# Filling a kernel's ramp with dummy matmuls, two elevenths of the first input on the instruction rings, weight sums on VectorE, and the last tile's store on its own queue

## The chip, the cores and the metric

The kernel runs on one core of a Trainium2 chip (trn2). The time is the device time of one execution in microseconds; a quoted time is a median over several executions. On one core all runs of this study were in the ordinary (fast) state, so no slow runs enter. A trace comes from one profiled execution, whose span is about 1.7 us shorter than the device time of the same run; positions in time ("at 15.4") are microseconds from the start of that trace.

The engines are TensorE (PE in the profile; PEld is its weight load), VectorE (DVE), ScalarE (ACT), GpSimd (POOL) and SyncE (SP). SP, ACT and POOL each issue DMAs on a queue of their own; those of SP and ACT are called the instruction rings here. Input 0 is divided into eleven groups for loading, its "elevenths". The matmuls write to tiles in PSUM, a memory that this program divides into eight banks; a "tag" is a pool of it with a fixed number of buffers.

## The reference

For each of 8 inputs of 2496 x 256: a real Fourier transform over the sequence, a complex 256 x 256 product with bias, a soft threshold, the inverse transform; then a mixture of experts that picks one expert per input and applies two matrix products.

```python
X = np.fft.rfft(x, axis=1)                       # 8 x 2496 x 256
Yr = X.real @ w_r - X.imag @ w_i + b_r
Yi = X.real @ w_i + X.imag @ w_r + b_i
Yr = sign(Yr) * maximum(abs(Yr) - 0.01, 0)       # Yi the same
y  = np.fft.irfft(Yr + 1j * Yi, n=2496, axis=1)
e_idx = argmax(y.mean(axis=1) @ w_gate, axis=1)  # one expert for each input
out = gate_w * (maximum(y @ w1[e], 0) @ w2[e])
```

## The kernel before

Everything is laid out by a small list scheduler inside the kernel: every operation is given a cost and a virtual time, and the scheduler emits the instructions of each engine in the order that its model finds best. It is a model; on the chip the order stays as emitted, whatever the real times are.

The parts that the change touches, with cuts:

```python
BANKS = {"a": 5, "h": 2, "o": 1}          # PSUM banks for each tag: "o" has one
...
warm = cpool.tile([P, 512], FP16, name="warm")
nc.vector.memset(warm, 0.0)
x0_part(nc.sync, 0, 0, 2, xf)             # input 0, elevenths 0-1, instruction rings
x0_part(nc.scalar, 1, 0, 2, xf)
x0_part(nc.sync, 2, 0, 2, xf)
nc.scalar.dma_start(out=wa, in_=d_wa.ap())
x0_part(nc.sync, 0, 2, 4, xf)             # elevenths 2-3, instruction rings
...
for c0, c1 in ((4, 8), (8, 11)):          # the rest: GpSimd's queue, casting DMA
    for j in range(3):
        x0_part(nc.gpsimd, j, c0, c1, xin0)
...                                       # w_r and w_i behind it, same queue
pw = psum.tile([P, 512], FP32, tag="o", name="po", bufs=BANKS["o"])
for _ in range(WARM):                     # WARM = 9: raise TensorE's clock
    nc.tensor.matmul(pw, warm[:, 0:P], warm)
...
def bank(nm, tag):                        # a NEW buffer of the tag at each call
    return psum.tile([P, 512], FP32, tag=tag, name=nm, bufs=BANKS[tag])
...
def w_products(_):                        # the sums of the complex product
    nc.gpsimd.tensor_sub(out=w4[:, :, 0], in0=wm, in1=wr)
    nc.gpsimd.tensor_scalar_mul(out=wr, in0=wr, scalar1=-1.0)
    nc.gpsimd.tensor_sub(out=w4[:, :, 1], in0=wr, in1=wm)
```

Names in the profile: `pa` is the first transform stage (from `xin`, evacuated to `XB`), `pm` the "weight product" in the frequency domain of the first two inputs (a transform stage against the weights), `Pt`/`pb` what follows, `z`, `cl`, `Y` VectorE's bias and soft threshold, `pv` and `pi` the inverse transform, `ph` and `po` the two products of the expert, `ost` the output tile. The first two inputs go through this way, the other six through a slightly different one.

Of the kernel before, what the change touches and what calls it, by code (L numbers as in the profile page):

```python
# [11 lines left out]
FP32 = mybir.dt.float32  # L12
AFT = mybir.ActivationFunctionType
ALU = mybir.AluOpType
# [3 lines left out]
B = 8  # L18
# [69 lines left out]
PEN = 0.2  # L88
SLACK = 2.5


class Op:
    def __init__(self, engs, occ, lat, emit, vt, deps, allocs, dma):
        self.engs, self.occ, self.lat, self.emit = engs, occ, lat, emit
        self.vt, self.deps, self.allocs, self.dma = vt, deps, allocs, dma
        self.done = self.after = None
        self.slack = SLACK

# [8 lines left out]
class Schedule:  # L107
# [54 lines left out]
    def run(self):  # L162
        free = dict.fromkeys(("PE", "ACT", "DVE", "SP", "POOL"), 4.0)
        free["POOL"] = 17.0
        ring = {"SP": 7.0, "POOL": 25.0}
        todo = sorted(self.ops, key=lambda o: o.vt)
        self.log = []
        while todo:
            best = None
            seen = {e: 0 for e in free}  # L170
            for o in todo:
                if all(seen[e] > 24 for e in o.engs):
                    continue
                r = self.ready(o)
                if r is None:
                    continue
                for e in o.engs:
                    seen[e] += 1
                    s = max(r, free[e])
                    if e == "DVE" and len(o.engs) > 1:  # L180
                        s += PEN
                    k = (s, o.vt, s + o.lat[e])
                    if best is None or k < best[0]:
                        best = (k, o, e)
            (s, _, _), o, e = best
            if e == "DVE" and len(o.engs) > 1:
                s -= PEN
            todo.remove(o)
            for k in o.allocs:
                self.hist.setdefault(k.tag, []).append(k)  # L190
            free[e] = s + o.occ[e]
            o.done = s + o.lat[e]
            if o.dma:
                other = "POOL" if e == "SP" else "SP"
                t = max(ring[e], s + 1.3)
                behind = max(0.0, ring[other] - t)
                if e == "SP":
                    ext = min(2.3 * o.dma, behind)
                    ring[other] += ext / 2.3
                else:  # L200
                    ext = min(0.43 * o.dma, behind)
                    ring[other] += min(2.3 * behind, o.dma)
                ring[e] = t + o.dma + ext
                o.done = ring[e] + o.slack
            self.log.append((s, e, o))
            o.emit(e)
# [3 lines left out]
def kernel(  # L210
# [29 lines left out]
    XROW = 2 * D + 16  # L240
    WARM = 9
    BUFS = {"XT": 2, "hs": 2, "z": 3, "V": 6}
# [19 lines left out]
    def load_now(b, cuts, hold=None):  # L262
# [18 lines left out]
        "p g c -> p (g c)")[:, 0 : NG * D].rearrange("p (g c) -> p g c", c=2 * D)  # L281
    xf = hpool.tile([117, 4, 2 * D], FP32, name="hs")
    xv = x[0].rearrange("(a n) c -> a n c", n=N2)
    XH = ((0, 2), (2, 4))

# [7 lines left out]
    nc.vector.memset(warm, 0.0)  # L293
    x0_part(nc.sync, 0, 0, 2, xf)
    x0_part(nc.scalar, 1, 0, 2, xf)
    x0_part(nc.sync, 2, 0, 2, xf)
    nc.scalar.dma_start(out=wa, in_=d_wa.ap())
    x0_part(nc.sync, 0, 2, 4, xf)
    x0_part(nc.scalar, 1, 2, 4, xf)
    x0_part(nc.sync, 2, 2, 4, xf)  # L300
    for c0, c1 in ((4, 8), (8, 11)):
        for j in range(3):
            x0_part(nc.gpsimd, j, c0, c1, xin0)
# [3 lines left out]
    nc.gpsimd.dma_start(out=wm, in_=w_i.rearrange("(t p) c -> p t c", p=P))  # L307

    pw = psum.tile([P, 512], FP32, tag="o", name="po", bufs=BANKS["o"])
    for _ in range(WARM):  # L310
        nc.tensor.matmul(pw, warm[:, 0:P], warm)
    tf = cpool.tile([P, NK1, P], FP16, name="tf")
# [20 lines left out]
    e0 = cpool.tile([P, 1], FP16, name="e0")  # L333
    nc.sync.dma_start(out=e0, in_=d_e0.ap())
    wg = cpool.tile([P, 2, E], FP32, name="wg")
    nc.sync.dma_start(out=wg, in_=moe_w_gate.rearrange("(t p) e -> p t e", p=P))
    iot = cpool.tile([P, E], FP32, name="iot")
    nc.sync.dma_start(out=iot, in_=d_iota.ap())
    wi = cpool.tile([120, 117], FP16, name="wi")
    nc.sync.dma_start(out=wi, in_=d_wi.ap())  # L340
    wg16 = cpool.tile([P, 2, E], FP16, name="wg16")
    xin1 = load_now(1, (0, NG // 2))


    X0_AT, X1_AT = (4.3, 5.6, 8.8, 10.5), 25.0
    W_AT, T_AT = 11.2, (13.0, 15.5, 18.0)

# [5 lines left out]
    COPY = {"ACT": nc.scalar.copy, "DVE": nc.vector.tensor_copy}  # L353
    DIRECT = 2
    HOLD = 9
    LATE = -0.12
    PERIOD, SPAN, SHIFT = 49.5, 1.4, 0.6

    def bank(nm, tag):
        return psum.tile([P, 512], FP32, tag=tag, name=nm, bufs=BANKS[tag])  # L360
# [14 lines left out]
    def w_products(_):  # L375

        nc.gpsimd.tensor_sub(out=w4[:, :, 0], in0=wm, in1=wr)
        nc.gpsimd.tensor_scalar_mul(out=wr, in0=wr, scalar1=-1.0)
        nc.gpsimd.tensor_sub(out=w4[:, :, 1], in0=wr, in1=wm)
    w_late = S.op("POOL", 4.0, w_products, 1.0, deps=list(w_in))  # L380

    def wg_cast(eng):
        COPY[eng](out=wg16, in_=wg)
    wg_in = S.evac(20, wg_cast, 0.5, deps=[S.fixed(12.0)])
    t_in = [S.fixed(T_AT[0 if k1 < 4 else 1 if k1 < 12 else 2])
# [5 lines left out]
    def x_cast(c):  # L391
        def emit(eng):
            COPY[eng](out=xin0[:, c], in_=xf[:, c])
        return S.evac(500, emit, -30 + c, deps=[S.fixed(X0_AT[c // 2])])

    x_cast_ops = [x_cast(c) for c in range(4)]
    c1, c2 = [S.fixed(X0_AT[2])], [S.fixed(X0_AT[3])]
    xdone = {0: [x_cast_ops[:2], x_cast_ops[2:], c1, c1, c2, c2],
             1: [S.fixed(X1_AT)]}
# [499 lines left out]
    def add_moe(b, y_ops, yk, gate):  # L899
        w, gb_op, wk = gate  # L900
        v0 = b * PERIOD
        for c, (ns, nl) in enumerate(NCH):
# [32 lines left out]
            for sp in range(2):  # L935
                tago = "o" if b < B - 1 else "h"
                ok = S.tok(tago, BANKS[tago])
                oc = {}
                for q in range(4):
                    v = v0 + PERIOD * (c * 8 + 6 + 4 * sp + q) / 44  # L940

                    def mm(_, sp=sp, q=q, nl=nl, cell=cell, oc=oc, tag=tago):
                        if q == 0:
                            oc["p"] = bank("po", tag).rearrange(
                                "p (i c) -> p i c", i=2)
                        i = q // 2
                        s0 = min((2 * sp + i) * P, nl - P)
                        for ft in range(4 * (q % 2), 4 * (q % 2) + 4):
# [7 lines left out]
                             after=m2 if q else None,  # L956
                             allocs=[ok] if q == 0 else [])
                    m2 = m
                    hk.rel.append(m)
                    wk.rel.append(m)  # L960

                def ev(eng, oc=oc):
# [4 lines left out]
                    else:  # L967
                        nc.vector.tensor_scalar_mul(out=ost, in0=oc["p"],
                                                    scalar1=gbc_t[b])
                e = S.evac(560, ev, v, deps=[m2, gb_op])  # L970
                ok.rel.append(e)

                def st(_, ns=ns, nl=nl, sp=sp, oc=oc):
# [7 lines left out]
                    else:  # L981
# [3 lines left out]
                                          in_=ost[64:P, 1, :])  # L985
                S.op("SP", 0.3, st, v, deps=[e], dma=0.75)

# [34 lines left out]
```

## Time and profile before

| | before |
|---|---|
| time, median (range) | 441.28 us (441.0 to 441.76) |
| TensorE busy | 424.7 us, 96% of the span |
| first weight product of input 0 starts | 15.37 |
| tenth z (input 0 through the threshold) | 36.12 |
| first weight product of input 1 | 39.38 |
| first expert product | 57.15 |
| last matmul ends, kernel ends | 437.2, 441.3 |

These positions are starts read from the timeline.

The busy time of each engine by windows, before. Each line has the window, its length, then busy time and (in brackets) instruction count of TensorE, its weight load, VectorE, ScalarE and GpSimd, then the granted TensorE clock, the DMA share and the rate:

```profile
core 0: us, PE busy (x) PEld busy (x) DVE busy (x) ACT busy (x) POOL busy (x), PEclk, DMA share, GB/s
0.00:12.00 12.00, 6.03 (x31) 2.84 (x32) 1.98 (x5) 3.48 (x5) 6.57 (x15) 0.87 0.81 169
12.00:20.00 8.00, 6.99 (x42) 4.36 (x41) 3.15 (x6) 5.64 (x14) 7.50 (x12) 0.56 0.98 314
...
60.00:441.00 381.00, 375.93 (x3056) 272.39 (x3053) 250.44 (x512) 286.87 (x552) 21.99 (x32) 1.00 0.78 180
```

After 60 us TensorE has hardly a gap (375.9 of 381). What can be gained lies in the first 60 us and in the tail. From 12 to 20 us the granted clock is 0.56 on average.

TensorE in the first 16 us, before (start, length, engine, line and operation, tiles, count; the bracket is the idle time ahead of it and what ended it):

```profile
1.31 4.02 PE L311 MATMUL po<-warm 128*128 128x512 f16 x9 [1.31 <-DVE warm L293]
7.62 0.59 PE L478 MATMUL pa<-wa,xin 117*128 117x120 f16 x8 [2.29 <-ACT xin L393]
10.58 3.78 PE L478 MATMUL pa<-wa,xin 117*128 117x120 f16 x36 [2.37 <-DVE xin L393]
15.37 1.01 PE L514 MATMUL pm<-w,XB 128*128 128x512 f16 x2 [1.01 <-ACT w L364]
```

Nine dummies run from 1.31, done by 5.3, and then TensorE waits for data. The clock goes up at 5.35 and falls back at 8.76, so the first weight products run at half clock. That gap is what the change wants to fill.

The timeline of VectorE, and then that of GpSimd, from 19 to 25 us, before:

```profile
...
20.30 0.37 DVE L565 TENSOR_SCALAR cl<-z 128x512 f16<-128x512 f16 x1
20.71 0.80 DVE L567 TENSOR_TENSOR Y<-z,cl 128x512 f16<-128x512 f16 x1
...
22.36 1.26 DVE L565 TENSOR_SCALAR cl<-z 128x512 f16<-128x512 f16 x1
...
```

```profile
...
19.21 1.30 POOL L377 TENSOR_TENSOR w<-ost 128x512 f16<-128x512 f32 x1
20.61 1.51 POOL L378 TENSOR_SCALAR ost<-ost 128x512 f32<-128x512 f32 x1
22.21 1.26 POOL L379 TENSOR_TENSOR w<-ost 128x512 f16<-128x512 f32 x1
```

While GpSimd makes the weight sums, one `cl` takes 1.26 us and one `Y` 0.80; undisturbed ones take 0.29 and 0.42.

The end of the chain of waits, before (start, length, what; ACTq is ScalarE's sequencer, "issue" a time in which the engine waited for nothing that the profile shows):

```profile
435.95 1.22 PE po L949 x11
437.17 0.03 ACTq L965
437.19 0.05 issue
437.24 0.69 ACT ost L965
```

After the last matmul there is one cast of 0.69 us, then two stores; the span ends 4.1 us after the last matmul.

### The profile page before, as it was taken

What the parts mean: (1) busy time and instruction counts of PE and PEld (TensorE: products, weight loads), DVE (VectorE), ACT (ScalarE), POOL (GpSimd) and SP (SyncE); (2) the same over time, 40 slices, a digit from 0 to 9 for tenths busy, and PEclk for the clock granted to TensorE, in tenths of its full rate; (3) what the DMA queues carried; (4) which work ended last, traced back from release to release, by engine and by line L of the source; (5) the groups of instructions that cost most, each with busy time, mean ns of one, the idle gap of its engine ahead of it and who ended that gap; (6) DMA issues with size and microseconds to landing.
All of it is one profiled execution on the core that took longest, in us unless ns stands there. A gap on an engine that the chain in (4) does not pass through costs nothing.

```text
span 441.3 us, 9023 instructions
## 1 busy us (share of the span) xinstructions
PE 424.7 (96%) x3387; PEld 300.9 (68%) x3387; DVE 288.9 (65%) x605; ACT 328.6 (74%) x636; POOL 45.2 (10%) x69
## 2 busy tenths in 40 slices
PE   4888999999999999999999999999999999999996
PEld 1555566677677866778677876778667787676764
DVE  1496965298866787687966887678976877322110
ACT  2787887777967778777867778677777778678674
POOL 5920300021000200020000200020000010000000
PEclk8698999999999999999999999999999999999999
DMA  7998996899979988699988999699978456472222
GB/s 166 276 183 176 170 211 162 239 207 206 202 230 213 186 174 220 199 199 215 189 256 193 177 189 220 219 199 197 188 211 230 127 134 126 130 161 67 71 73 91
DMA packets 98961, 80.31 MB, mean 182 GB/s; under 512 B 8000, under 2 KB 91889, under 8 KB 98917
## 3 DMA queue, kind: packets, MB, share of 16 engines
q1 hardware_dynamic: 75499, 58.17, 48.9%
q0 software_dynamic: 23184, 21.22, 30.3%
q8 instruction: 26, 0.43, 0.4%
q10 hardware_dynamic: 234, 0.35, 0.3%
q14 instruction: 18, 0.15, 0.1%
HBM read 59.36 MB, written 38.80 MB: 222 GB/s over the span
## 4 chain that ended last, share of the span: by engine, by line
PE 77%; DVE 9%; DMA 7%; ACT 3%; issue 2%; SPq 1%; POOL 0%; ACTq 0%; POOLq 0%; DVEq 0%
PE po L949 28%; PE ph L917 26%; PE pm L693 8%; PE pi L788 3%; PE pa L591 3%; PE pv L436 3%; DMA xin<-in_x_dram 3%; PE px L655 3%; PE pm L514 2%; DMA V<-scr 2%; DVE z L556 2%; DMA hs<-in_x_dram 2%; DVE Y L567 1%; DVE cl L565 1%; DVE Y L735 1%
## 5 line engine op out<-in xcount | busy, mean ns | idle before, releaser
L929 ACT ACTIVATE hs<-ph 128x512 f16<-128x512 f32 (+1 forms) x296 | 170.2, 592 | 73.6 <-PE ph L917 68.4
L949 PE MATMUL po<-w2s,hs 128*128 128x256 f16 x1280 | 180.6, 272 | 0.0
L917 PE MATMUL ph<-ysb,w1s 128*128 128x512 f16 (+1 forms) x640 | 179.8, 374 | 0.5 <-ACT ysb L809 0.5
L949 PEld LDWEIGHTS <-hs 128*128 128x128 f16 x1280 | 123.3, 98 | 51.7 <-issue 2.2
L917 PEld LDWEIGHTS <-w1s 128*128 128x128 f16 x640 | 61.4, 98 | 21.5 <-issue 0.7
L965 ACT ACTIVATE ost<-po,gbc 128x512 f32<-128x512 f32 x78 | 53.7, 689 | 13.0 <-PE po L949 13.0
L735 DVE TENSOR_TENSOR Y<-z,cl 64x512 f16<-64x512 f16 x120 | 50.4, 420 | 2.8
L707 DVE TENSOR_TENSOR tt<-pm,bias 128x512 f16<-128x512 f32 x60 | 38.6, 684 | 19.4 <-PE pm L693 19.4
L693 PE MATMUL pm<-w,XT 128*128 128x256 f16 x360 | 50.0, 273 | 0.4
L693 PEld LDWEIGHTS <-XT 128*128 128x128 f16 x360 | 34.2, 98 | 12.8 <-DVE XT L674 3.8
L931 DVE TENSOR_SCALAR hs<-ph 128x512 f16<-128x512 f32 (+1 forms) x24 | 16.5, 686 | 38.5 <-PE ph L917 33.8
L716 DVE TENSOR_TENSOR z<-pm,tt 128x512 f16<-128x512 f32 x60 | 38.4, 679 | 2.9 <-PE pm L693 2.9
L444 ACT CAST V<-pv 128x512 f16<-128x512 f32 x55 | 32.5, 612 | 2.1 <-PE pv L436 1.5
L803 DVE CAST ysb<-pi 128x468 f16<-128x468 f32 (+1 forms) x41 | 23.0, 582 | 16.8 <-PE pi L788 16.5
L663 DVE CAST XT<-px 128x512 f16<-128x512 f32 x32 | 21.6, 689 | 16.5 <-PE px L655 16.3
L601 ACT CAST A<-pa 120x512 f16<-120x512 f32 x50 | 28.1, 603 | 1.3 <-PE pa L591 1.1
L436 PE MATMUL pv<-Y,ti 128*128 128x256 f16 x160 | 25.9, 272 | 2.5 <-DVE Y L567 2.1
L803 ACT CAST ysb<-pi 128x468 f16<-128x468 f32 (+1 forms) x55 | 25.8, 534 | 2.3 <-PE pi L788 2.2
L514 PE MATMUL pm<-w,XB 128*128 128x512 f16 x80 | 24.7, 428 | 1.9 <-ACT w L364 1.0
L525 ACT CAST Pt<-pm 128x512 f16<-128x512 f32 x35 | 19.9, 589 | 6.7 <-PE pm L514 6.7
L788 PEld LDWEIGHTS <-V 120*128 120x128 f16 x352 | 21.0, 98 | 4.0 <-issue 0.7
L788 PE MATMUL pi<-wi,V 120*128 120x117 f16 x352 | 23.2, 214 | 0.3
(70 smaller groups left out, 332.8 us busy)
## 6 DMA issues: line engine op xcount, KB each, us to landing
out_dram<-ost SPq DMA_DIRECT2D x72, 256.0 KB
scr<-V SPq DMA_DIRECT2D x80, 128.0 KB
V<-scr SPq DMA_DIRECT2D x24, 420.0 KB
xin<-in_x_dram POOLq DMA_DIRECT2D x21, 429.0 KB, 9.3
XB<-fwd SPq DMA_DIRECT2D x30, 256.0 KB
fwd<-A SPq DMA_DIRECT2D x18, 360.0 KB
w1s<-in_moe_w_dram POOLq DMA_DIRECT2D x8, 512.0 KB, 8.3
w2s<-in_moe_w_dram POOLq DMA_DIRECT2D x8, 512.0 KB, 7.8
```

What stands on the lines that cost most here:

```text
L436: nc.tensor.matmul(pv[:, D * i : D * i + D], ti[:, k0 + i, :], cell["Y"](i))
L514: nc.tensor.matmul(pm, A_t[b]["A"][:, ch, k1, :, :], w4[:, ch, 2:4, :].rearrange("p t c -> p (t c)"), start=(ch == 0), stop=(ch == 1))
L693: nc.tensor.matmul(pm[:, D * a : D * a + D], cell["X"][:, ch, a, t].rearrange("p i k -> p (i k)"), w4[:, ch, t, :], start=(ch == 0), stop= ...
L707: nc.vector.tensor_add(out=cell["tt"][:, r], in0=cell["T", 2].rearrange("p (a c) -> p a c", a=2), in1=bias[:, r].unsqueeze(1).to_broadcast ...
L716: nc.vector.tensor_add(out=cell["z"][:, r], in0=cell["T", 1 - r].rearrange("p (a c) -> p a c", a=2), in1=cell["tt"][:, r])
L735: nc.vector.tensor_sub(out=Y[64 * r : 64 * r + 64, :, i], in0=cell["z"][s, r], in1=cell["cl"][s, r])
L788: nc.tensor.matmul(pi[:, 117 * i : 117 * i + M], V2[:, g, ch * P : ch * P + P], w)
L803: COPY[eng](out=yv[:, :, 12 * gb : 12 * gb + 3 * nf].rearrange("p a (g j) -> p a g j", j=3), in_=pi[:, 0 : 117 * nf].rearrange("p (g a j) ...
L917: nc.tensor.matmul(ph[:, 0:nl], w1s_t[b][:, ch, fc * P : fc * P + P], ysb_t[b][:, ch, ns : ns + nl], start=(ch == 0), stop=(ch == 1))
L929: nc.scalar.activation(out=o, in_=i, func=AFT.Relu)
L949: nc.tensor.matmul(oc["p"][:, i, :], cell["hs"][:, ft, s0 : s0 + P], w2s_t[b][:, ft, :], start=(ft == 0), stop=(ft == E - 1))
L965: nc.scalar.activation(out=ost, in_=oc["p"], func=AFT.Copy, scale=gbc_t[b])
```

## The change

Its intent has four parts: (1) only two elevenths of input 0 stay on the instruction rings and the rest comes in one ordered stream on GpSimd's queue; (2) the scheduler may put dummy matmuls into any gap of TensorE until 50 us, so that the clock stays up; (3) the weight sums move from GpSimd to VectorE; (4) the last output tile is cast in halves, by VectorE and ScalarE, and ScalarE's queue issues its last store. The core of the diff, with cuts:

```diff
-    WARM = 9
+    XF = 2
+    X0_CUTS = ((2, 6), (6, 9), (9, 11))
...
-    x0_part(nc.sync, 0, 2, 4, xf)
-    x0_part(nc.scalar, 1, 2, 4, xf)
-    x0_part(nc.sync, 2, 2, 4, xf)
-    for c0, c1 in ((4, 8), (8, 11)):
+    nc.scalar.copy(out=warm[0:1, 0:1], in_=warm[0:1, 1:2])
+    for c0, c1 in X0_CUTS:
...
-    pw = psum.tile([P, 512], FP32, tag="o", name="po", bufs=BANKS["o"])
-    for _ in range(WARM):
-        nc.tensor.matmul(pw, warm[:, 0:P], warm)
...
-        nc.gpsimd.tensor_sub(out=w4[:, :, 0], in0=wm, in1=wr)
-        nc.gpsimd.tensor_scalar_mul(out=wr, in0=wr, scalar1=-1.0)
-        nc.gpsimd.tensor_sub(out=w4[:, :, 1], in0=wr, in1=wm)
+        nc.vector.tensor_sub(out=w4[:, :, 0], in0=wm, in1=wr)
+        nc.vector.scalar_tensor_tensor(out=w4[:, :, 1], in0=wr, scalar=-1.0,
+                                       in1=wm, op0=ALU.mult, op1=ALU.subtract)
...
+    for _ in range(WARM):                       # WARM = 100, until 50.0 us
+        def dummy(_):
+            nc.tensor.matmul(bank("po", "o"), warm[:, 0:P], warm)
+        dk = S.tok("o", BANKS["o"])
+        o = S.op("PE", 0.216, dummy, 1e6, allocs=[dk])
+        dk.rel.append(o)
+        o.until = WARM_END
...
+                if last:     # last output tile: own bank for its second half
+                    e = S.op("DVE", 0.45, ev_first, v, deps=[m1, gb_op])
+                    e = S.op("ACT", 0.45, ev_last, v, deps=[m2, e])
```

The scheduler's new cost table also starts its engines at other times, and four small loads move to a later place on SyncE. A new copy of one element on ScalarE brings its table load to the start.

More of the change, by code (lines that the diff above doesn't have):

```diff
@@ L89 @@
 SLACK = 2.5
+IDLE = 0.2
 class Op:
@@ L96, in __init__ @@
         self.done = self.after = None
-        self.slack = SLACK
+        self.slack, self.until = SLACK, None
 class Tok:
@@ L162, in run @@
     def run(self):
-        free = dict.fromkeys(("PE", "ACT", "DVE", "SP", "POOL"), 4.0)
-        free["POOL"] = 17.0
-        ring = {"SP": 7.0, "POOL": 25.0}
+        free = dict.fromkeys(("PE", "ACT", "DVE", "SP", "POOL"), 1.3)
+        free["ACT"], free["POOL"] = 4.5, 17.0
+        ring = {"SP": 7.0, "POOL": 26.0}
         todo = sorted(self.ops, key=lambda o: o.vt)
         self.log = []
-        while todo:
+        while any(not o.until for o in todo):
             best = None
@@ L174, in run @@
                 r = self.ready(o)
-                if r is None:
+                if r is None or (o.until and max(r, free["PE"]) > o.until):
                     continue
@@ L181, in run @@
                         s += PEN
+                    if o.until:
+                        s += IDLE
                     k = (s, o.vt, s + o.lat[e])
@@ L187, in run @@
                 s -= PEN
+            if o.until:
+                s -= IDLE
             todo.remove(o)
@@ L281 @@
         "p g c -> p (g c)")[:, 0 : NG * D].rearrange("p (g c) -> p g c", c=2 * D)
-    xf = hpool.tile([117, 4, 2 * D], FP32, name="hs")
+    xf = hpool.tile([117, 4, 2 * D], FP32, name="hs")[:, 0:XF]
     xv = x[0].rearrange("(a n) c -> a n c", n=N2)
-    XH = ((0, 2), (2, 4))
     def x0_part(eng, j, c0, c1, dst):
@@ L293 @@
     nc.vector.memset(warm, 0.0)
-    x0_part(nc.sync, 0, 0, 2, xf)
-    x0_part(nc.scalar, 1, 0, 2, xf)
-    x0_part(nc.sync, 2, 0, 2, xf)
+    x0_part(nc.sync, 0, 0, XF, xf)
+    x0_part(nc.scalar, 1, 0, XF, xf)
+    x0_part(nc.sync, 2, 0, XF, xf)
     nc.scalar.dma_start(out=wa, in_=d_wa.ap())
-    x0_part(nc.sync, 0, 2, 4, xf)
-    x0_part(nc.scalar, 1, 2, 4, xf)
-    x0_part(nc.sync, 2, 2, 4, xf)
-    for c0, c1 in ((4, 8), (8, 11)):
+    nc.scalar.copy(out=warm[0:1, 0:1], in_=warm[0:1, 1:2])
+    for c0, c1 in X0_CUTS:
         for j in range(3):
@@ L333 @@
     e0 = cpool.tile([P, 1], FP16, name="e0")
-    nc.sync.dma_start(out=e0, in_=d_e0.ap())
     wg = cpool.tile([P, 2, E], FP32, name="wg")
-    nc.sync.dma_start(out=wg, in_=moe_w_gate.rearrange("(t p) e -> p t e", p=P))
     iot = cpool.tile([P, E], FP32, name="iot")
-    nc.sync.dma_start(out=iot, in_=d_iota.ap())
     wi = cpool.tile([120, 117], FP16, name="wi")
-    nc.sync.dma_start(out=wi, in_=d_wi.ap())
     wg16 = cpool.tile([P, 2, E], FP16, name="wg16")
     xin1 = load_now(1, (0, NG // 2))
-    X0_AT, X1_AT = (4.3, 5.6, 8.8, 10.5), 25.0
-    W_AT, T_AT = 11.2, (13.0, 15.5, 18.0)
+    X0_AT, X1_AT = (5.6, 8.0, 9.3, 10.3), 26.0
+    W_AT, T_AT = 11.6, (14.0, 16.2, 18.4)
     S = Schedule()
@@ L354 @@
     DIRECT = 2
+    WARM, WARM_END = 100, 50.0
     HOLD = 9
@@ L375, in w_products, with small_loads @@
     def w_products(_):
-        nc.gpsimd.tensor_sub(out=w4[:, :, 0], in0=wm, in1=wr)
-        nc.gpsimd.tensor_scalar_mul(out=wr, in0=wr, scalar1=-1.0)
-        nc.gpsimd.tensor_sub(out=w4[:, :, 1], in0=wr, in1=wm)
-    w_late = S.op("POOL", 4.0, w_products, 1.0, deps=list(w_in))
+        nc.vector.tensor_sub(out=w4[:, :, 0], in0=wm, in1=wr)
+        nc.vector.scalar_tensor_tensor(out=w4[:, :, 1], in0=wr, scalar=-1.0,
+                                       in1=wm, op0=ALU.mult, op1=ALU.subtract)
+    w_late = S.op("DVE", 1.4, w_products, -24.9, deps=list(w_in))
+    def small_loads(_):
+        nc.sync.dma_start(out=e0, in_=d_e0.ap())
+        nc.sync.dma_start(out=wg, in_=moe_w_gate.rearrange("(t p) e -> p t e", p=P))
+        nc.sync.dma_start(out=iot, in_=d_iota.ap())
+        nc.sync.dma_start(out=wi, in_=d_wi.ap())
+    small = S.op("SP", 1.6, small_loads, -30, deps=[S.fixed(10.0)], lat=4.0)
+    for _ in range(WARM):
[5 more added lines that the diff above has]
+        o.until = WARM_END
     def wg_cast(eng):
         COPY[eng](out=wg16, in_=wg)
-    wg_in = S.evac(20, wg_cast, 0.5, deps=[S.fixed(12.0)])
+    wg_in = S.evac(20, wg_cast, 0.5, deps=[small])
     t_in = [S.fixed(T_AT[0 if k1 < 4 else 1 if k1 < 12 else 2])
@@ L393, in emit @@
             COPY[eng](out=xin0[:, c], in_=xf[:, c])
-        return S.evac(500, emit, -30 + c, deps=[S.fixed(X0_AT[c // 2])])
-    x_cast_ops = [x_cast(c) for c in range(4)]
-    c1, c2 = [S.fixed(X0_AT[2])], [S.fixed(X0_AT[3])]
-    xdone = {0: [x_cast_ops[:2], x_cast_ops[2:], c1, c1, c2, c2],
+        return S.evac(500, emit, -30 + c, deps=[S.fixed(X0_AT[0])])
+    x_cast_ops = [x_cast(c) for c in range(XF)]
+    c1, c2, c3 = ([S.fixed(t)] for t in X0_AT[1:])
+    xdone = {0: [x_cast_ops, c1, c1, c2, c3, c3],
              1: [S.fixed(X1_AT)]}
@@ L937, in add_moe @@
                 ok = S.tok(tago, BANKS[tago])
+                last = b == B - 1 and c == 4 and sp == 1
+                ok2 = S.tok(tago, BANKS[tago])
                 oc = {}
@@ L940, in add_moe, with mm @@
                     v = v0 + PERIOD * (c * 8 + 6 + 4 * sp + q) / 44
-                    def mm(_, sp=sp, q=q, nl=nl, cell=cell, oc=oc, tag=tago):
-                        if q == 0:
-                            oc["p"] = bank("po", tag).rearrange(
-                                "p (i c) -> p i c", i=2)
+                    def mm(_, sp=sp, q=q, nl=nl, cell=cell, oc=oc, tag=tago,
+                           last=last):
+                        if q == 0 or q == 2 and last:
+                            oc["p"] = oc["p", q // 2] = bank(
+                                "po", tag).rearrange("p (i c) -> p i c", i=2)
                         i = q // 2
@@ L956, in add_moe @@
                              after=m2 if q else None,
-                             allocs=[ok] if q == 0 else [])
-                    m2 = m
+                             allocs=[ok] if q == 0 else [ok2]
+                             if q == 2 and last else [])
+                    m1, m2 = (m if q == 1 else m1 if q else None), m
                     hk.rel.append(m)
@@ L969, in ev @@
                                                     scalar1=gbc_t[b])
-                e = S.evac(560, ev, v, deps=[m2, gb_op])
-                ok.rel.append(e)
                 def st(_, ns=ns, nl=nl, sp=sp, oc=oc):
@@ L985, in st, with ev_last, ev_first @@
                                           in_=ost[64:P, 1, :])
-                S.op("SP", 0.3, st, v, deps=[e], dma=0.75)
+                def ev_last(_, ns=ns, nl=nl, sp=sp, oc=oc):
+                    r0 = ns + 256 * sp
+                    ost = oc["o"]
+                    nc.scalar.activation(
+                        out=ost[64:P, 1], in_=oc["p", 1][64:P, 1],
+                        func=AFT.Copy, scale=gbc_t[b][64:P])
+                    nc.scalar.dma_start(out=out[b, r0 + P : ns + nl, :],
+                                        in_=ost[64:P, 1, :])
+                def ev_first(_, ns=ns, sp=sp, oc=oc):
+                    r0 = ns + 256 * sp
+                    oc["o"] = ost = opool.tile([P, 2, D], FP32, name="ost")
+                    nc.vector.tensor_scalar_mul(
+                        out=ost[:, 0], in0=oc["p", 0][:, 0], scalar1=gbc_t[b])
+                    nc.sync.dma_start(out=out[b, r0 : r0 + P, :],
+                                      in_=ost[:, 0, :])
+                if last:
+                    e = S.op("DVE", 0.45, ev_first, v, deps=[m1, gb_op])
+                    ok.rel.append(e)
+                    e = S.op("ACT", 0.45, ev_last, v, deps=[m2, e])
+                    ok2.rel.append(e)
+                else:
+                    e = S.evac(560, ev, v, deps=[m2, gb_op])
+                    ok.rel.append(e)
+                    S.op("SP", 0.3, st, v, deps=[e], dma=0.75)
     for b in range(B):
```

## The prediction

> **What bounds the kernel.** After 60 us TensorE does: the windows table gives it 375.9 of 381 us busy to 441. The first 60 us are a ramp: from the matmuls' widths about 20 us of TensorE time are lost there. In the chain of waits the ramp is input 0's DMA (8.2 us, the second ring piece lands at 10.1), half-clock TensorE (granted clock 0.5 from 8.8 to 19.0), then VectorE's z/cl/Y sequence from 19.6 to 51, broken by eight half-clock matmuls at 39.4 (3.5 us). The first weight product starts at 15.37, after the casts of the last input piece (12.9) and of the weights (landed 14.26). The tail: last matmul ends 437.2, cast 0.69, two stores 0.42 apart, end 441.3.
>
> **Intended gain.** Input 0 in one ordered stream: first weight product about 1.5 us sooner and at full clock (-1.8). POOL's three weight sums (19.2 to 23.5) go: while they ran one cl took 1.26 us instead of 0.29 and one Y 0.80 instead of 0.42, so -1.4 on VectorE's chain; the Trainium skill, "SBUF — State Buffer" (SBUF: two separate sides), calls the shared port pair an exclusive lock, and these durations agree. Cold stretch at 39 avoided: -1.8. Tail: smaller cast, no second issue: -0.7. Together about -7.
>
> **What I think spoils it.** The instruction order of the changed kernel shows two things the diff hides.
> 1. The first dummy waits for the new ScalarE copy, which writes the tile the dummies read and stands behind two DMA issues and the table load (1.28 us): dummies start near 3.4 us, not 1.3.
> 2. Every dummy takes a new buffer of the one-bank "o" tag, so 44 of the 56 wait for completion of the matmul just before. The nine old ones shared one tile, without waits. In this trace a 512-column matmul completes 0.648 us after its start at half clock, 0.394 at full; with about 0.05 for the wait, a dummy costs an estimated 0.70 or 0.44 us, not the 0.216 that the schedule assumes.
>
> 38 dummies stand before the first weight product, in order on TensorE. If the clock is raised by 9 us, that product starts near 24 (+9); if it stays at half, near 31 to 34 (+16 to +19). The Trainium skill, "TensorE: Matmul & The Clock Gate" (Part 1), has the clock raised after a busy window of about 3.4 us; here changes fall on multiples of 3.41 us, a window 64% filled did not raise it and one 93% filled did. Serialized dummies fill 61%: probably not enough. Against this stand the -1.4, -0.7 and part of the other savings; the seven dummies before the second group of inverse products cost another 1 to 2.
>
> **Prediction.** 452 us, 80% range 434 to 461. Faster by over 2%: 0.10; within 2%: 0.40; slower: 0.50.
>
> **What would show it.** Dummies 0.65 to 0.70 us (cold) or about 0.44 (warm) apart, each released by TensorE itself; first dummy released by ScalarE near 3.4; granted clock low during them; first weight product at 24 to 34; VectorE idle until then. Right in any case: no cl over 0.5 us near the start, end about 3.4 us after the last matmul instead of 4.1.
>
> **What would make it wrong.** If a wait on the engine's own completion costs nothing, dummies stand 0.216 apart and the time is 433 to 437. If 61% filling raises the clock, and it stays up, the loss is only about 4 to 6 us.

## The result, and the profile after

The changed kernel takes 454.66 us (median of 4 runs, 453.89 to 454.94) against 441.52 (441.0 to 442.19) for the kernel before in the same rounds: a ratio of 1.0294, 95% interval 1.0274 to 1.0314, slower. (A ratio is the mean time of one kernel's fast runs over that of the other's of the same rounds, so it is not quite the ratio of the medians.)

Section 1 of the page, first before, then after (busy us, share of the span, instructions):

```profile
PE 424.7 (96%) x3387; PEld 300.9 (68%) x3387; DVE 288.9 (65%) x605; ACT 328.6 (74%) x636; POOL 45.2 (10%) x69
```

```profile
PE 439.8 (97%) x3434; PEld 304.0 (67%) x3434; DVE 289.4 (64%) x610; ACT 327.5 (72%) x633; POOL 42.4 (9%) x69
```

TensorE is busier in the slower kernel. The Trainium skill, "Trainium Kernel Development and Optimization" (Performance Expectations), calls matmul busy time a bad metric for how close a kernel is to its limit; here it goes from 96% to 97% while the time grows by 3%. The busy share of the weight load, which that page prefers, falls from 68% to 67%, the right direction but small. The mean granted clock looks better too, 0.997 instead of 0.985, but it is taken only from the first clock record on, which comes at 23.52 after and at 5.35 before. The matmuls ahead of it ran at half clock; with that stretch counted as 0.5, I estimate 0.971 after and 0.979 before. So neither the busy share nor the printed mean clock shows the loss.

The windows after, for the same stretches:

```profile
0.00:12.00 12.00, 7.84 (x14) 1.49 (x15) 0.70 (x2) 2.10 (x3) 7.70 (x18) 1.00 0.76 139
12.00:20.00 8.00, 7.43 (x20) 2.00 (x19) 0.66 (x1) 0.56 (x1) 6.98 (x12) 1.00 0.98 327
...
70.00:453.00 383.00, 376.78 (x3059) 272.83 (x3057) 252.08 (x514) 286.96 (x553) 22.04 (x32) 1.00 0.77 179
```

Look at the counts: up to 12 us TensorE is busy 7.84 us with only 14 matmuls, and from 12 to 20 us with 20. Before it was 6.03 us for 31, and 6.99 for 42. VectorE and ScalarE have almost nothing to do from 12 to 20 us. (The clock of 1.00 in the first two lines is not what TensorE had: the trace has no clock record before 23.5 us, and the matmuls run at half speed there.) After the ramp the kernel is as before.

TensorE in the first 30 us, after:

```profile
3.44 14.69 PE L388 MATMUL po<-warm 128*128 128x512 f16 x23 [3.44 <-ACT warm L303]
17.92 1.00 PE L490 MATMUL pa<-wa,xin 117*128 117x120 f16 x8
18.72 3.19 PE L388 MATMUL po<-warm 128*128 128x512 f16 x5
21.70 1.80 PE L490 MATMUL pa<-wa,xin 117*128 117x120 f16 x16
...
25.71 2.54 PE L388 MATMUL po<-warm 128*128 128x512 f16 x6
28.09 1.89 PE L526 MATMUL pm<-w,XB 128*128 128x512 f16 x8
```

The first dummy is released at 3.44 by ScalarE's copy, which stands behind a table load of 1.28 us. The first 23 take 14.69 us, 0.64 each. The data of input 0 was complete at 13.25 and the weights at 14.57, but TensorE takes the dummies in its order, and the first weight product starts at 28.09. From the chain of waits of the first 70 us, after:

```profile
3.44 0.62 PE po L388
4.10 0.60 PE po L388
...
17.54 0.58 PE po L388
18.12 0.80 PE pa L490 x8
```

Each dummy is a step of the chain of its own, and no other engine stands between them: each waits for the one before. The starts, 0.64 apart, are the measurement; the ends of matmuls are modelled in such a trace.

VectorE's first steps, after:

```profile
31.17 0.29 DVE L577 TENSOR_SCALAR cl<-z 128x512 f16<-128x512 f16 x1
31.50 0.42 DVE L579 TENSOR_TENSOR Y<-z,cl 128x512 f16<-128x512 f16 x1
...
32.78 0.28 DVE L577 TENSOR_SCALAR cl<-z 128x512 f16<-128x512 f16 x1
```

The slow `cl` and `Y` are gone. And the end of the chain, after:

```profile
...
446.95 0.70 ACT ost L981
...
447.69 1.05 PE po L964 x8
448.73 0.03 ACTq L1005
448.76 0.33 issue
449.08 0.47 ACT ost L1005
```

Here a new wait appears: the last eight matmuls wait for a PSUM bank that ScalarE's cast frees (TensorE is idle 0.39 us in its timeline at that place).

Where the 11.5 us between the two traces arise:

| start of | before | after | after later by |
|---|---|---|---|
| first dummy | 1.31 | 3.44 | 2.13 |
| first weight product, input 0 | 15.37 | 28.09 | 12.72 |
| first z | 19.58 | 30.45 | 10.87 |
| tenth z | 36.12 | 45.66 | 9.54 |
| first weight product, input 1 | 39.38 | 49.77 | 10.39 |
| eleventh z (first of input 1) | 43.62 | 52.37 | 8.75 |
| first expert product | 57.15 | 66.97 | 9.82 |
| output matmul 1120 | 405.66 | 416.68 | 11.02 |
| end | 441.31 | 452.78 | 11.47 |

(Output matmul 1120 is the first of the last input's 160, counted from 0 and without dummies; the expectations call it the 1120th.)

12.7 us are lost before the first weight product; 1.9 come back because the clock is up there, 1.3 because GpSimd no longer disturbs VectorE, 1.6 because the stretch of input 1's first weight products is not at half clock. Dummies in later gaps take some again: four of them stand before input 1's first weight product (48.26 to 49.77) and seven between two groups of inverse products (62.20 to 65.01). Between the first expert product and output matmul 1120 another 1.2 us are lost, which I did not trace further; the last 0.45 are in the tail.

### The profile page after: what moved, and what is told of

It reads as the page before. It is cut to its first block, busy times and chain, and to the rows that moved or that the text cites. A ratio compares the mean times of both kernels' runs of the same rounds, so it can differ in the third digit from the quotient of the medians.

```text
span 452.8 us, 9118 instructions
## 1 busy us (share of the span) xinstructions
PE 439.8 (97%) x3434; PEld 304.0 (67%) x3434; DVE 289.4 (64%) x610; ACT 327.5 (72%) x633; POOL 42.4 (9%) x69
## 4 chain that ended last, share of the span: by engine, by line
PE 81%; DVE 9%; DMA 5%; issue 2%; ACT 1%; POOL 0%; SPq 0%; ACTq 0%; POOLq 0%; DVEq 0%
PE po L964 28%; PE ph L929 25%; PE pm L705 7%; PE po L388 5%; PE pi L800 3%; DMA xin<-in_x_dram 3%; PE pv L448 3%; PE pa L603 3%; PE px L667 2%; DMA V<-scr 2%; PE pm L526 2%; DVE z L568 2%; DVE Y L747 1%; DVE Y L579 1%; DVE cl L577 1%
## 5 line engine op out<-in xcount | busy, mean ns | idle before, releaser
L388 PE MATMUL po<-warm 128*128 128x512 f16 x56 | 27.1, 484 | 6.2 <-ACT warm L303 3.4
```

What stands on the lines that cost most here:

```text
L388: nc.tensor.matmul(bank("po", "o"), warm[:, 0:P], warm)
```

## The experiments

Twelve kernels ran, five rounds each; all gave correct results. The kernel before: 442.43, 441.77 and 441.74 us. By the rule of 2% only the changed kernel is slower, e3 is unclear, and all others are the same as the kernel before; so the differences below, of 1 to 4 us, have to be weighed against the ranges of the times.

The theory: the loss is the wait of each dummy for the completion of the one just before, because each takes a new buffer of a tag with one bank. Rivals: the late start behind ScalarE's copy; the number of dummies as such; the reordered loads or the moved weight sums.

### e1_shared: all dummies in one tile

```diff
+    o_now = {"t": None}
     def bank(nm, tag):
-        return psum.tile([P, 512], FP32, tag=tag, name=nm, bufs=BANKS[tag])
+        t = psum.tile([P, 512], FP32, tag=tag, name=nm, bufs=BANKS[tag])
+        if tag == "o":
+            o_now["t"] = t if nm == "pd" else None
+        return t
...
-            nc.tensor.matmul(bank("po", "o"), warm[:, 0:P], warm)
+            if o_now["t"] is None:
+                bank("pd", "o")
+            nc.tensor.matmul(o_now["t"], warm[:, 0:P], warm)
```

> The changed kernel, but its 56 dummy matmuls write one shared tile as long as no real tile takes the bank, so that none waits for the dummy before it. Number, place and operands of all matmuls are the same. Theory W (the wait of each dummy for its predecessor's completion is the loss): dummies stand 0.427 us apart at half clock and 0.216 at full, the clock is raised between 6.9 and 10.3 us, the first weight product starts at 15.7 to 17.4 us instead of 28.1, and the time falls from 454.7 to 441 to 444. Rival N (the 56 extra matmuls or the other parts of the change are the loss): the first weight product stays later than 22 us and the time stays over 449.

Measured: 440.44 us (440.21 to 441.09), ratio 0.9965 (0.9946 to 0.9984). The instruction order of every engine is that of the changed kernel; only the waits are gone. TensorE's timeline of this run:

```profile
3.44 7.07 PE L395 MATMUL pd<-warm 128*128 128x512 f16 x23 [3.44 <-ACT warm L303]
10.35 0.58 PE L497 MATMUL pa<-wa,xin 117*128 117x120 f16 x8
...
15.91 1.89 PE L533 MATMUL pm<-w,XB 128*128 128x512 f16 x8
```

The same 23 dummies from the same start take 7.07 us instead of 14.69: 0.427 apart until the clock goes up at 7.40, then 0.216. The first weight product is at 15.91. The time is a little under the expected 441 to 444. The changed kernel loses 13.1 us to the kernel before, and without the waits 14.2 us of medians come back, so all of the loss hangs on these waits (the two medians are of different calls, and the kernel before moved by 0.9 between them).

### e2_shared_early and e3_early_only: the copy ahead of the dummies

e2 is e1 and gives ScalarE's copy a tile of its own, so that the first dummy does not wait for it; e3 has that edit alone, with each dummy in a new buffer as in the changed kernel.

```diff
-    nc.scalar.copy(out=warm[0:1, 0:1], in_=warm[0:1, 1:2])
+    tl = cpool.tile([1, 2], FP16, name="tl")
+    nc.vector.memset(tl, 0.0)
+    nc.scalar.copy(out=tl[0:1, 0:1], in_=tl[0:1, 1:2])
```

> As e1_shared, and the ScalarE copy that brings the table load forward works on a tile of its own, so that the first dummy does not wait for it. Theory W with theory S (the first dummy's wait for ScalarE costs too): first dummy at 1.3 us instead of 3.4, the first weight product then waits for the weights' casts (landed at 14.6) and starts at 15.2 to 15.8; time 439.5 to 441.5. Rival: the start does not matter because everything up to 15 waits for DMA: same time as e1_shared within 0.5 us.

> The changed kernel with its waiting dummies, and only the ScalarE copy moved to a tile of its own. Theory W: the chain of dummies keeps its pitch of 0.64 us at half clock and only starts 2.1 us sooner, so the time falls by 1.5 to 3 us, to 451.5 to 453. If the first dummy's wait for ScalarE were the main loss, the time would fall below 446.

Measured: e2 440.73 us (439.57 to 443.05), e3 450.31 (450.16 to 450.75). In both the first dummy starts at 1.32. In e2 the first weight product is at 14.77, 1.1 us sooner than in e1, and the time is the same, as the rival had it. What was won at the start is lost again at 29.8, where TensorE stands 2.56 us until the last part of input 1 has landed (32.5). (Such stops are taken here from start to start, less the 0.216 of one matmul; the timeline, with its modelled ends, shows 0.16 less.) In e3 the gain is 4.4 us, more than I expected (451.5 to 453), and about 2.1 was to be had by the earlier start alone: the clock went up at 17.15 and not at 23.52. So the late copy is worth 4.4 us as long as the dummies wait, and how much of it depends on when the clock goes up; without the waits (e1 against e2) it is worth nothing measurable.

### e4_no_dummies: the change without any dummy

```diff
-            nc.tensor.matmul(bank("po", "o"), warm[:, 0:P], warm)
+            pass
```

> The changed kernel without any dummy matmul, the nine of before gone too; all other instructions stand in the same order. Theory W: the rest of the change is harmless. First weight product at 15.3 to 15.6 us, at half clock, z about 19.6, VectorE's chain 1.3 us shorter than before because POOL no longer computes, a second half-clock stretch near 38: time 439.5 to 441.5. Rival D (the new order of input 0's DMA costs): weights land later than 16 us and the time is over 444.

Measured: 440.86 us (439.33 to 441.97), ratio 0.997 (0.9947 to 0.9993), the same as e1 and e2. TensorE's timeline of this run:

```profile
14.98 3.35 PE L526 MATMUL pm<-w,XB 128*128 128x512 f16 x8 [0.96 <-ACT w L360]
```

Here the first weight products take 3.35 us, at half clock; in e1 they take 1.89. The 1.5 us are visible in the ramp (first z at 18.80, against 18.27 in e1 and 17.28 in e2) and do not reach the time. So well made dummies are worth nothing measurable here. In this run the clock rose at 17.97 and stayed up at 38 without any dummy, where I had expected a second half-clock stretch.

The kernel before shows the same without an edit. Of its 33 runs, 18 have a mean clock of 0.982 to 0.992, with a fall of the clock as in the trace above, and 15 have 0.996 or more, which leaves room for a fall at the very end alone. Their mean times are 442.0 and 442.1 us (standard errors 0.20 and 0.25). So a clock that does not fall back was worth nothing measurable in that kernel either (e9 below shows where the lead can go).

### e5_x1_wide, e6_tail_bank, e7_all: what e2 gives back, and the tail

e5 is e2 with input 1 loaded into unpadded rows, so that its DMA has fewer, longer pieces (2960 packets on GpSimd's queue in the first 45 us, 4400 in e2). e6 is e1 with a free bank for the second half of the last output tile. e7 has both.

```diff
 e5
+        if b == 1:
+            xin = xin.rearrange("p g c -> p (g c)")[:, 0 : NG * D].rearrange(
+                "p (g c) -> p g c", c=2 * D)
 e6
-                ok2 = S.tok(tago, BANKS[tago])
+                ok2 = S.tok("o", BANKS["o"])
-                                "po", tag).rearrange("p (i c) -> p i c", i=2)
+                                "po", "o" if q == 2 else tag).rearrange(
+                                    "p (i c) -> p i c", i=2)
```

> As e2_shared_early, but input 1 is loaded without the padding between its rows in SBUF, so that its packets are as wide as those of input 0; the order of all instructions is the same. In e2_shared_early TensorE waited 2.56 us near 30 us for the last part of input 1 (landed at 32.5). Theory L (once the dummies' waits are gone, the landing of input 1 caps the ramp): it lands before 31, that wait shrinks under 0.7 us, and the time falls by 1 to 2 us against e2_shared_early, to 438.7 to 439.8. Rival: the cap is VectorE's chain or a later load, and the time stays within 0.4 us of e2_shared_early.

> As e1_shared, but the second half of the last output tile takes the bank that is free at the end instead of one of the two that the tiles before it use; the order is the same. In the changed kernel TensorE stood 0.39 us before that half until ScalarE had emptied the tile before. Expected: that idle time is gone and the kernel ends 0.4 us sooner after the first of the last 160 output matmuls; time 440.0 against 440.4 of e1_shared. Rival: ScalarE is still busy with the tile before, so nothing is won.

> e2_shared_early with the wider packets of input 1 and the free bank for the last half tile. If both hold and add: 438.2 to 439.4, 0.8 percent under before. If the ramp's gain is lost again in later loads: about 440.

Measured: 440.59, 440.42 and 440.80 us. e5 did cut the wait near 30 us from 2.56 to 0.61 (and 0.41 more for VectorE), yet the time did not follow, and the expected 438.7 to 439.8 is missed, as is e7's 438.2 to 439.4; its tenth z is at 33.24, one us sooner than in e2 (34.28), but later output matmuls stand level (the 161st at 108.66 and 108.61). In e5's trace the lead over e2 is 1.45 us at the first transform of input 1, 0.24 at 36 us and gone at 48: between, TensorE waits for ScalarE's V (0.34 and 0.31 idle in the timeline) and VectorE's Y (0.58). So there the limit passes from the load to VectorE and ScalarE, as the rival expectation had it. Some traces also have a later stop near 106 us for the load of a later input (1.18 us in e6, 1.87 in e4), but e1, e2 and e5 have none. e6 took the bank stall out, as meant: from output matmul 1120 to the end it has 35.80 us instead of 36.12 in e1. The gain of 0.3 is below the scatter of the times. That the ramp's gains are lost at later waits, for loads in some traces and for VectorE and ScalarE in e5, fits these traces; no run isolates it.

### e8_sums_pool: weight sums back on GpSimd

e8 is e1 with the three lines of the weight sums on GpSimd as in the kernel before.

> As e1_shared, but the weight sums go back to POOL, as before the change. Theory P (POOL's sums slow VectorE's chain): while they run one or two of the cl and Y operations take 0.8 to 1.3 us instead of 0.3 to 0.4, the tenth z comes 1.0 to 1.4 us later than in e1_shared (33.5), and the time rises by 0.7 to 1.4 us. Rival: the chain has slack by then (it waits for DMA), and the time stays within 0.4 us.

Measured: 443.53 us (442.79 to 444.54), ratio 1.0039 (1.0018 to 1.006). VectorE in this run:

```profile
19.78 1.20 DVE L584 TENSOR_SCALAR cl<-z 128x512 f16<-128x512 f16 x1
21.01 0.80 DVE L586 TENSOR_TENSOR Y<-z,cl 128x512 f16<-128x512 f16 x1
...
22.66 1.26 DVE L584 TENSOR_SCALAR cl<-z 128x512 f16<-128x512 f16 x1
```

From first to tenth z e8 needs 17.4 us and e1 15.2. In time e8 is 3.1 us above the 440.42 of e6, which differs from e1 only in the tail; 0.8 of it is already there at the first weight product (16.69 against 15.91). That part fits the moment at which the clock goes up, which the edit does not set: 8.97 in e8's trace and 7.40 in e1's, and 6.41 and 6.17 in those of e6 and e12, whose first weight products are at 15.43 and 15.36. The 3.1 are more than the 0.7 to 1.4 us I had expected; with the sooner ramp two `cl` meet the sums here (1.20 and 1.26), and in the kernel before one. The Trainium skill, "SBUF — State Buffer" (SBUF: two separate sides), has VectorE and GpSimd share a port pair by exclusive lock, with the loser blocked for a whole instruction; the 1.20 to 1.26 us against 0.29 undisturbed agree. This part of the change pays.

### e9_before_23 and e10_before_23_wait: the wait alone, in the kernel before

These start from the kernel before, with nothing of the change: 23 dummies instead of 9. In e9 they share one tile, in e10 each takes a new buffer.

```diff
-    WARM = 9
+    WARM = 23
 e10 also
-    pw = psum.tile([P, 512], FP32, tag="o", name="po", bufs=BANKS["o"])
     for _ in range(WARM):
+        pw = psum.tile([P, 512], FP32, tag="o", name="po", bufs=BANKS["o"])
         nc.tensor.matmul(pw, warm[:, 0:P], warm)
```

> The kernel before, with 23 dummy matmuls instead of 9 at the start, still into one shared tile and so without waits. Theory (the wait is the cost, not the count): dummies 0.427 us apart until the clock is raised, then 0.216; the last one ends at 8 to 9 us, before input 0 is there; first weight product within 0.5 us of before's 15.4; time within 1.5 us of before. Rival (the number of dummies itself delays the ramp): first weight product later by 3 us or more and the time with it.

> The same 23 dummies in the kernel before, but each asks the pool for a new buffer of the one-bank tag, as the changed kernel does. Nothing else of the change is in it. Theory (each waits for the completion of the one just before): dummies 0.64 us apart at half clock, the last ends near 16.0 us, the input's transform follows at half clock, first weight product near 21 us or later, time 4 to 7 us over the run with shared tile (446 to 449). Rival (the wait alone is harmless and something else in the changed kernel is slow): same as the run with shared tile within 1 us.

Measured: e9 441.41 us (441.27 to 442.24), e10 444.20 (443.18 to 445.09); the kernel before 441.74. TensorE's timeline, first e9, then e10:

```profile
1.31 7.94 PE L311 MATMUL po<-warm 128*128 128x512 f16 x23 [1.31 <-DVE warm L293]
...
15.20 1.02 PE L514 MATMUL pm<-w,XB 128*128 128x512 f16 x4 [1.19 <-ACT w L364]
```

```profile
1.31 10.21 PE L311 MATMUL po<-warm 128*128 128x512 f16 x16 [1.31 <-DVE warm L293]
...
15.07 2.00 PE L478 MATMUL pa<-wa,xin 117*128 117x120 f16 x32
18.59 1.89 PE L514 MATMUL pm<-w,XB 128*128 128x512 f16 x8 [1.52 <-ACT w L364]
```

Fourteen more dummies without waits cost nothing. They gain nothing either, though e9's clock stays up from 7.02 and its first z is 1.9 us sooner than before (17.70): more of VectorE's work then meets GpSimd's weight sums (`cl` of 2.21 and 1.26 us, a `Y` of 0.80), and the tenth z is at 36.26, level with 36.12 before. The same dummies with the wait stand 0.64 apart (16 of them in 10.2 us) and delay the first weight product by 3.4 us and the time by 2.8. The direction and the pitch are as expected; the size I had put at 4 to 7 us and 21 us is missed, because here matmuls of the transform run between the last seven dummies (the loop issues all 23 first, but the trace has them in this order, so e10 differs from e9 in TensorE's order too), a window of the clock is full enough (0.91 by the reckoning at the end), and the clock goes up at 13.67, before most of the transform. The rival "number of dummies" falls.

### e11_rings4: input 0 back on the rings as before

e11 is e2 with four elevenths of input 0 on the instruction rings; the scheduler then places one dummy more.

```diff
-    XF = 2
-    X0_CUTS = ((2, 6), (6, 9), (9, 11))
+    XF = 4
+    X0_CUTS = ((4, 8), (8, 11))
...
+    x0_part(nc.sync, 0, 2, 4, xf)
+    x0_part(nc.scalar, 1, 2, 4, xf)
+    x0_part(nc.sync, 2, 2, 4, xf)
```

> The changed kernel with shared dummy tile and early start (440.7 us), but four elevenths of input 0 on the instruction rings as before, in two pieces each. My prediction gave the ordered stream about 1.5 us at the first weight product. If that holds, the weights' last part lands 1 us or more later than 14.1, the first weight product stands 1 us or more later than 14.8, and the time is 1 to 2 us over 440.7. If the split of input 0 does nothing, as the landings of before (14.26) and of this kernel (14.08) suggest, the weights land within 0.4 us of 14.1 and the time is within 0.7 us of 440.7.

Measured: 439.32 us (438.64 to 440.21), ratio 0.9943 (0.9916 to 0.9969). The first weight product is at 14.82, in e2 at 14.77: nothing gained by the new split there. But the time is 1.4 us under e2's and 1.5 under e12's, which neither expectation had. It is the fastest kernel, and faster than both kernels compared here. TensorE at the first transform of input 1, first e2, then e11:

```profile
32.57 0.59 PE L499 MATMUL pa<-wa,xin 117*128 117x120 f16 x8 [2.40 <-DMA xin<-in_x_dram]
```

```profile
30.57 0.58 PE L502 MATMUL pa<-wa,xin 117*128 117x120 f16 x8 [0.40 <-DMA xin<-in_x_dram]
```

Input 1 lands 2.0 us sooner in e11. It stands behind input 0 in GpSimd's queue. With four elevenths on the rings GpSimd issues six pieces of input 0 and not nine, and input 1's pieces are issued 0.7 us sooner (from 16.4 instead of 17.1). So the part of the change that was to help input 0 may delay what follows, but this is not shown: e3, with the new split, issues them from 17.07 and has them at 29.65, sooner than e11 (30.43). One trace each and overlapping intervals of the ratios (e2 has 0.9942 to 0.9998) are thin support; e1 and e12 show that the landing of input 1 also differs without any edit near it (TensorE has no wait over 0.25 us there in e1, and one of 1.23 in e12). Why e11 is the fastest stays open.

### e12_old_tail: the last tile as before

e12 is e1 with the last output tile handled as in the kernel before.

```diff
-                last = b == B - 1 and c == 4 and sp == 1
+                last = False
```

> The changed kernel with shared dummy tile (440.4 us), but the last output tile handled as before (two casts on ScalarE, both stores as before, no wait for its bank). Theory (the new tail costs 0.46 us): from the 1120th output matmul to the end 35.65 us instead of 36.12, time 0.2 to 0.6 us below 440.4. Rival (the prediction's term, a gain of 0.7 us by the new tail): time 0.7 us above.

Measured: 440.86 us (439.42 to 441.51), e1 had 440.44. From output matmul 1120 to the end: 36.11 us, and 36.12 in e1. Both expectations miss: the new tail neither costs nor gains. The end of e12's chain:

```profile
434.70 0.03 ACTq L988
434.73 0.33 issue
435.05 0.69 ACT ost L988
```

The cast takes 0.69 again instead of 0.47, and the span ends 4.60 us after the last matmul, against 4.06 in e1. So the new handling does shorten what follows the last matmul, by 0.54; it gives this back at the bank: the last matmul ends 32.06 us after output matmul 1120 in e1, and 31.51 in e12 and in e6, which has a free bank (and ends 4.29 after it). In front of the last cast stand 0.33 us, where the kernel before has 0.05. In all eleven traces of the changed kernel's family these 0.33 us stand before the 832nd instruction in ScalarE's record (waits for semaphores counted). In e11 that is the cast before, at 431.65, and its last cast waits only 0.05. So they go with a place in ScalarE's instruction stream and not with the new tail; I do not know their cause. Together with the landing of the last store this is why the tail of the kernel before, 35.65, is not reached by e12.

All times once more, with the first weight product of input 0 (one trace each; its place also moves with the moment the clock goes up, by 1.3 us between e12 and e8):

| kernel | median us | ratio to before, 95% | first weight product |
|---|---|---|---|
| changed | 454.66 | 1.0294 (1.0274 to 1.0314) | 28.09 |
| e3 early start, waits kept | 450.31 | 1.0188 (1.0167 to 1.0209) | 24.33 |
| e10 before, 23 dummies, waits | 444.20 | 1.0054 (1.0026 to 1.0081) | 18.59 |
| e8 shared tile, sums on GpSimd | 443.53 | 1.0039 (1.0018 to 1.006) | 16.69 |
| e9 before, 23 dummies, no waits | 441.41 | 0.999 (0.9965 to 1.0016) | 15.20 |
| e4 no dummies | 440.86 | 0.997 (0.9947 to 0.9993) | 14.98 |
| e12 shared tile, old tail | 440.86 | 0.9972 (0.9944 to 0.9999) | 15.36 |
| e7 e2 + e5 + e6 | 440.80 | 0.9974 (0.9954 to 0.9994) | 15.41 |
| e2 shared tile, early start | 440.73 | 0.997 (0.9942 to 0.9998) | 14.77 |
| e5 e2, input 1 unpadded | 440.59 | 0.997 (0.9945 to 0.9996) | 15.20 |
| e1 shared tile | 440.44 | 0.9965 (0.9946 to 0.9984) | 15.91 |
| e6 e1, free bank at the end | 440.42 | 0.9966 (0.9948 to 0.9984) | 15.43 |
| e11 e2, four elevenths on the rings | 439.32 | 0.9943 (0.9916 to 0.9969) | 14.82 |

## Why the prediction was right or wrong

The predicted time, 452.0 us, lies 2.7 below the measured 454.66; the range and the direction hold. That says little by itself: the range is 27 us wide, and "slower" had a probability of 0.50. The closeness is in part luck, since 452 lies between two cases of the clock, and the clock rose between them for a reason I had not foreseen. What was right is the mechanism. Point by point:

- **The wait of each dummy for the one before: right, and without it there is no loss.** e1 takes it away with the instruction order unchanged and gets 14.2 us back; e10 puts it into the kernel before and loses 2.8, where e9 with as many dummies loses nothing. The pitch was estimated at 0.70 us at half clock and 0.44 at full, and measured 0.64 and 0.43. The Trainium skill, "TensorE: Matmul & The Clock Gate" (Single matmul latency), gives the time of one isolated matmul, from which one works out an estimate of 0.609 us for 512 columns at half clock and 0.379 at full; the measured pitches are 0.03 and 0.05 above that. At half clock this is nearer than my 0.70, at full clock my 0.44 was nearer. (By the trace 43 dummies stand directly behind another, where I had counted 44.)
- **The late first dummy: right.** 3.44 us, released by ScalarE. e2 and e3 start at 1.32. While the dummies wait it is worth 4.4 us (e3).
- **The clock: in between.** "Serialized dummies fill 61%: probably not enough" held while there were only dummies: such windows did not raise it. It rose at 23.5, in a window that also held the transform. So the first weight product is at 28.09, between the two cases of 24 and 31 to 34.
- **The weight sums off GpSimd, -1.4: right.** From the first to the tenth z the changed kernel needs 1.33 us less than before; e8 against e1 shows 2.2.
- **The cold stretch at 39, -1.8: right in size** (-1.64 from the first weight product of input 1 to the eleventh z). The dummies need not be its cause: without any (e4) the clock stayed up there as well. That it is worth 1.8 us of the time is not shown; runs of the kernel before whose clock did not fall back were no faster.
- **First weight product 1.5 us sooner by the ordered stream: wrong.** Without dummies it is 0.4 sooner (e4), and e11, with the old split, has it at the same place as e2. The step that failed is that the ordered stream brings the weights sooner: they landed at 14.33 in e4 and 14.26 before (in the ten traces with the stream at 14.08 to 14.76, in the four with the old split at 13.96 to 14.39).
- **The tail, -0.7: wrong.** The terms "smaller cast, no second issue" are there (0.54 us less after the last matmul, e1 against e12), but the second half's matmuls wait for a bank. The sum is 0 (36.12 against 36.11). "End about 3.4 us after the last matmul" was measured at 4.05.
- **Seven dummies in the inverse products cost 1 to 2: right, at its lower edge.** 1.07 us from the eleventh z to the first expert product, where these seven stand; in e1, where they do not wait, that stretch is as long as before (13.51 and 13.53).
- **About -7 in all, had the waits cost nothing: wrong.** "433 to 437" was expected for unwaited dummies; e1 and e2 are at 440.4 to 440.7. The terms above shrink the sum, and what remains in the ramp is lost again in part at later waits: for the load of input 1 in e2, for VectorE and ScalarE in e5.

## What to carry to other kernels

A filler instruction must wait for nothing: look at what it allocates and what it reads, because a pool with one buffer turns a stream of matmuls 0.216 us apart into one of 0.43, and at half clock 0.427 into 0.64, and instructions that stand ahead in the order delay all that follows. A high busy share can come from fillers, and a mean clock can leave out the start of a trace, so judge a ramp by when the first useful instruction starts. And before raising the ramp's speed, find out what the next stage will wait for (a load in e2, VectorE and ScalarE in e5); here nearly 1.5 us won at the start came to nothing.

## What the Trainium skill lacked or had wrong

- "TensorE: Matmul & The Clock Gate" (Part 1) says the clock rises after a busy window of about 3.4 us, free-running; the runs agree with the window (changes of clock are multiples of 3.41 us apart). It gives no fill at which a window counts. From the starts and widths of the matmuls I estimate: windows filled 0.79 to 1.0 raised the clock, windows of 0.63 to 0.75 did not; windows of 0.12 and 0.37 lowered it, windows of 0.42 and more did not. (A window's fill is 0.427 or 0.216 us, by the clock, for each 512 columns of its matmuls.) So a stretch can lower the clock without any idle gap near the 3 us that the page names: in the window of 0.37, from 36.07 to 39.48 before, no two matmuls start more than 1.04 us apart.
- The same page gives the latency of a single matmul and the rate of a stream, but not the case between: a stream in which each matmul waits for the one before. Here that costs 0.64 us at half clock and 0.43 at full, instead of 0.427 and 0.216.
- "ScalarE: Activation LUTs" (What ACT_TABLE_LOAD costs) gives about 1283 ns and a drain of about 1380 ns for every switch to another set, and its step "Table-load gate" counts the drain for a first call too. Here the first load took 1.28 us and the copy behind it started at once (3.19 after a load from 1.89), without such a drain.
- No page that I read has the 0.33 us that ScalarE waits for nothing visible before its 832nd instruction, in all eleven traces of the changed kernel's family.

